# A convolution, gated token mixing and channel mixing kernel: full-width convolution matmuls, chunk stages placed by another slot, separate wave-sum tiles, fixed sum tiles

## The chip, the cores and the metric

One NeuronCore of a Trainium2 chip. The metric is the device time of the kernel in microseconds (us), the median of several executions. Instruction times come from one profiled execution of each kernel.

In the profile lines PE is TensorE, DVE VectorE, ACT ScalarE, POOL GpSimd and SP (SPq) the queue of SyncE; L424 is a line of the kernel.

## The reference

```python
# x: [8, 4224, 192]; weight: [8 heads, 7 taps]
w   = softmax(weight, over taps)
x   = causal depthwise convolution of x with w (24 channels per head)
theta = x @ w_theta                           # [192, 192]
zr, zi = x * cos(theta), x * sin(theta)
y   = w_tok_r @ zr + w_tok_i @ zi             # over tokens, [4224, 4224] each
u   = x + y
out = u + max(u @ w_ch, 0)                    # w_ch: [192, 192]
```

Nearly all the work is the two token products. The kernel does them in bf16, seven block products in place of eight per pair of row blocks (a scheme with sums of operands).

## The kernel before

A *chunk* is 128 tokens: it is convolved, transposed, multiplied with `w_theta` (the stage "theta"), turned into `zr` and `zi` ("wave"), and three sums of these are made for the seven products. Eleven chunks are resident in SBUF; 33 pass through. A *visit* is one pair of 128-row blocks of the output against the resident chunks: 14 series of 11 matmuls of 384 columns (8 series in an unpaired visit, of which there is one in every 17). Partial results go to DRAM in f32 quarters and come back in *sum tiles* `d`. Everything is issued in an order that the program works out beforehand from a model of time; the unit `n` in it is the time of one fourteenth (in an unpaired visit one eighth) of a visit, 1.79 us.

The convolution of a chunk, two 64-column halves side by side in one bank:

```python
for hh in range(2):
    h = 2 * hp + hh
    for half in range(2):
        pe(nc.tensor.matmul(
            pc[half * 2 * Q : (half + 1) * 2 * Q, hh * B * G : (hh + 1) * B * G],   # Q = 32
            lhsT=bands[:, h, :, :].rearrange("p a m -> p (a m)"),                   # 96 x 64
            rhs=self.xw[:, half, :, h * G : (h + 1) * G],                           # 96 x 192
            start=True, stop=True,
        ), B * G / 2)
```

The order of a late chunk's stages (cut), as offsets from the visit before its first:

```python
zr, zi = (10.05, 12.05) if pair(visits[v][0]) else (4.05, 8.05)
for at, fn in (
    (-4.0, lambda: chunks[c].conv(0)),
    ...                                         # conv(1), conv(2), conv(3) to -2.5
    (-2.4, lambda: c + 2 < NCH and load_chunk(c + 2)),
    (-2.0, lambda: chunks[c].transpose(0)),     # DMA transposes on the SP queue
    (-1.9, lambda: chunks[c].transpose(1)),
    (-1.8, lambda: chunks[c].keep()),
    (zr - 5.0, lambda: chunks[c].theta(0)),
    ...
    (zi + 2.0, lambda: (chunks[c].sum(2), chunks[c].sum(3))),
):
    events.append((t0 + at * n, fn))
```

The sums of weights S1 to S4 are made on VectorE out of transposed weights A11 to A22, at these slots of a visit (over 14: in the visit that uses them):

```python
SLOT = {"A11": 2.4, "A21": 4.4, "A22": 6.5, "A12": 8.5,
        "S3": 14.1, "S1": 14.6, "S2": 15.3, "S4": 17.1}
```

Sum tiles come from a rotating pool of seven; `tags` counts the free ones, and two more are added late:

```python
def load(self, q, tag):
    d = dpool.tile([P, HN], F32, name="d", tag="d") if tag is None else tag
    self.d[q], self.tag[q] = d, tag
    if self.first: return
    nc.sync.dma_start(out=d, in_=part[self.u][q][:, :])
    if self.v == residual_at[self.u]:
        ...            # some us later: GpSimd adds the residual, d = d + xr (128 x 768, f32)
tags = [None] * 7
def free_sums(tag): tags.append(tag); load_sums()
```

The finished rows are transposed by DMA (ACT queue) and multiplied with `w_ch` 11 us of model time later; only the last four visits transpose them on TensorE:

```python
outputs.append((pos[0] + 11.0, self, q, transposed(ub, False, uT)))
```

Of the kernel before, what the change touches and what calls it, by code (L numbers as in the profile page):

```python
# [11 lines left out]
BF16 = mybir.dt.bfloat16  # L12
# [4 lines left out]
def kernel(  # L17
# [22 lines left out]
    nc = tc.nc  # L40
# [36 lines left out]
    def pe(ins, cols=0):  # L77
        clock[0] += cols / 2400 + 0.0025
        return in_order("pe", ins)
# [10 lines left out]
    zpool = ctx.enter_context(tc.tile_pool(name="zpool", bufs=SLOTS))  # L90
    wpool = ctx.enter_context(tc.tile_pool(name="wpool", bufs=6))
    spool = ctx.enter_context(tc.tile_pool(name="spool", bufs=4))
    dpool = ctx.enter_context(tc.tile_pool(name="dpool", bufs=7))
    BANKS = {"y": 6, "mm": 2}
    psum = {
        k: ctx.enter_context(
# [61 lines left out]
        return (a * NCH + c) * Q  # L158


    wsb = constp.tile([P, H, KS], F32, name="wsb")
    nc.sync.dma_start(out=wsb, in_=weight.partition_broadcast(P))
    half_pi = constp.tile([P, 1], F32, name="half_pi")
    nc.gpsimd.memset(half_pi, math.pi / 2)
    bands = constp.tile([2 * WR, H, 2, Q], BF16, name="bands")

    def channel_weights(w, name):
        R = D - P
# [10 lines left out]
    class Chunk:  # L179
# [23 lines left out]
        def conv(self, hp):  # L203
            if hp == 0:
                self.xz = wk.tile([P, B, D], BF16, name="xz", tag="xz")
            pc = bank("mm", "pc")
            for hh in range(2):
                h = 2 * hp + hh
                for half in range(2):
                    pe(nc.tensor.matmul(  # L210
                        pc[half * 2 * Q : (half + 1) * 2 * Q,
                           hh * B * G : (hh + 1) * B * G],
                        lhsT=bands[:, h, :, :].rearrange("p a m -> p (a m)"),
                        rhs=self.xw[:, half, :, h * G : (h + 1) * G],
                        start=True, stop=True,
                    ), B * G / 2)
            act(nc.scalar.activation(  # L217
                out=self.xz[:, :, hp * 2 * G : (hp + 1) * 2 * G].rearrange(
                    "p b (h g) -> p h b g", h=2
                ),  # L220
                in_=pc[:, 0 : 2 * B * G].rearrange("p (h b g) -> p h b g", h=2, b=B),
                func=AT.Copy,
            ))
            if hp == H // 2 - 1:
                self.xf = self.xz[:, :, :].rearrange("p b d -> p (b d)")
                self.xT, self.ang = [], []

        def keep(self):
            for a in range(NQ):
# [33 lines left out]
            ))  # L263

        def sum(self, i):
            if i == 0:
                self.zt = zpool.tile(
                    [P, 3, HN], BF16, name="zt", tag="zt", bufs=SLOTS + 1
                )
                zs[self.c] = self  # L270
            near, far = slice(0, HN), slice(HN, N)
            t = [self.zt[:, k, :] for k in range(3)]
            o, p, q = (
                lambda: (t[0], self.zr[:, far], self.zr[:, near]),
                lambda: (t[1], self.zi[:, far], t[0]),
                lambda: (self.zr[:, far], self.zi[:, far], self.zr[:, far]),
                lambda: (t[2], self.zi[:, near], t[1]),
            )[i]()
            dve(nc.vector.tensor_tensor(out=o, in0=p, in1=q, op=ALU.subtract))

        def operand(self, i, g):
            near = slice(g * PC, (g + 1) * PC)
            far = slice(HN + g * PC, HN + (g + 1) * PC)
            return {
                "B11": lambda: self.zr[:, near], "T3": lambda: self.zr[:, far],
                "B21": lambda: self.zi[:, near], "B22": lambda: self.zi[:, far],
                "T1": lambda: self.zt[:, 0, near], "T2": lambda: self.zt[:, 1, near],
                "T4": lambda: self.zt[:, 2, near],
            }[i]()

    def transposed(u, by_pe, uT=None):
# [91 lines left out]
    class Visit:  # L383
        def __init__(self, v):
            self.v = v
            self.u, self.lo, self.hi = visits[v]
            self.first, self.final = firsts[v], finals[v]
            self.pair = pair(self.u)
            self.quarters = [3, 1, 0, 2] if self.pair else [1, 0]
            self.d, self.tag, self.missing = {}, {}, set()  # L390

        def load(self, q, tag):
            d = dpool.tile([P, HN], F32, name="d", tag="d") if tag is None else tag
            self.d[q], self.tag[q] = d, tag
            if self.first:
                return
            nc.sync.dma_start(out=d, in_=part[self.u][q][:, :])
            if self.v == residual_at[self.u]:
                self.missing.add(q)
                later(4.0, lambda: self.residual(q))  # L400
# [31 lines left out]
        def add(self, q, y, g, begins=False, ends=False):  # L432
            while q not in self.d or q in self.missing:
                if delayed:
                    delayed.pop(0)[2]()
                else:
                    output_step()
            o = self.d[q][:, g * PC : (g + 1) * PC]
            if self.first and begins:
                act(nc.scalar.activation(out=o, in_=y[:, 0:PC], func=AT.Copy))  # L440
            else:
                dve(nc.vector.tensor_tensor(out=o, in0=y[:, 0:PC], in1=o, op=ALU.add))  # L442
            if not (ends and g == NG - 1):
                return
            if self.final:
                self.output(q)
                return

            def store():
                nc.sync.dma_start(out=part[self.u][q][:, :], in_=self.d[q])  # L450
                stored.add((self.u, q, self.hi))
                later(8.0, lambda: free_sums(self.tag[q]))

            later(3.0, store)

# [70 lines left out]
        def output_end(self, q, uT):  # L526
            d = self.d[q]
            for k in range(2):
                dk = d[:, k * PC : (k + 1) * PC]
                dve(nc.vector.scalar_tensor_tensor(  # L530
                    out=dk, in0=channel_mix(uT, k, wch_[0]), scalar=0.0, in1=dk,
                    op0=ALU.max, op1=ALU.add,
                ))
            bs = slice(q % 2 * B // 2, (q % 2 + 1) * B // 2)

            def store():
                nc.sync.dma_start(
                    out=out[bs, self.rows(q), :].rearrange("b s d -> s b d"),
                    in_=d[:, :].rearrange("p (b d) -> p b d", d=D),
                )  # L540
                later(8.0, lambda: free_sums(self.tag[q]))

            later(2.0, store)

# [6 lines left out]
    def later(us, fn):  # L551
        delayed.append((pos[0] + us, len(made), fn))
        made.append(None)
        delayed.sort(key=lambda x: x[:2])

    made = []
    turn = [0]
    tags = [None] * 7
    order = [Visit(v) for v in sequence]
    waiting = [(vi, q) for vi in order for q in vi.quarters]  # L560

    def free_sums(tag):
        tags.append(tag)
        load_sums()
# [36 lines left out]
    for a, lo in ((0, True), (1, False)):  # L601
# [2 lines left out]
            channel_multiplier=-1 if lo else 1, base=WR - 1 if lo else -WR,  # L604
            compare_op=ALU.is_ge, fill=0.0,
        )
    wmax = constp.tile([P, H], F32, name="wmax")
    nc.vector.tensor_reduce(out=wmax, in_=wsb, axis=mybir.AxisListType.X, op=ALU.max)
    nc.vector.tensor_tensor(
        out=wsb, in0=wsb, in1=wmax[:, :].unsqueeze(2).to_broadcast([P, H, KS]),  # L610
# [1 line left out]
    )  # L612
    nc.scalar.activation(out=wsb, in_=wsb, func=AT.Exp)
    nc.scalar.activation(out=wmax[:, 0:1], in_=wsb[:, 0, 0:1], func=AT.Sin)
    wsum = constp.tile([P, H], F32, name="wsum")
    nc.vector.tensor_reduce(out=wsum, in_=wsb, axis=mybir.AxisListType.X, op=ALU.add)
    nc.vector.tensor_scalar_add(out=wsum, in0=wsum, scalar1=1e-9)
    wrcp = constp.tile([P, H], F32, name="wrcp")
    nc.vector.reciprocal(out=wrcp, in_=wsum)
    wbf = constp.tile([P, H, KS], BF16, name="wbf")  # L620
    nc.vector.tensor_tensor(
        out=wbf, in0=wsb, in1=wrcp[:, :].unsqueeze(2).to_broadcast([P, H, KS]),
        op=ALU.mult,
# [16 lines left out]
            )  # L640
    for a in range(2):
        nc.vector.tensor_scalar_mul(
            out=bands[:, :, a, :], in0=btmp[:, 0], scalar1=block[:, a : a + 1]
        )
    ident = constp.tile([P, P], BF16, name="ident")
    make_identity(nc, ident)
# [30 lines left out]
    def chunk_events(c, v):  # L677
        t0, n = starts[v], length(v) / parts(visits[v][0])
        zr, zi = (10.05, 12.05) if pair(visits[v][0]) else (4.05, 8.05)
        for at, fn in (  # L680
            (-4.0, lambda: chunks[c].conv(0)),
            (-3.5, lambda: chunks[c].conv(1)),
            (-3.0, lambda: chunks[c].conv(2)),
            (-2.5, lambda: (chunks[c].conv(3), c == NCH - 1 and last_conv())),
            (-2.4, lambda: c + 2 < NCH and load_chunk(c + 2)),
            (-2.0, lambda: chunks[c].transpose(0)),
            (-1.9, lambda: chunks[c].transpose(1)),
            (-1.8, lambda: chunks[c].keep()),
            (zr - 5.0, lambda: chunks[c].theta(0)),
            (zr - 2.7, lambda: chunks[c].theta(1)),  # L690
            (zr, lambda: chunks[c].wave(0, 0)),
# [4 lines left out]
            (zi + 0.05, lambda: chunks[c].wave(1, 1)),  # L696
            (zi + 0.7, lambda: chunks[c].times_x(1, 0)),
            (zi + 1.2, lambda: (chunks[c].times_x(1, 1), chunks[c].sum(1))),
            (zi + 2.0, lambda: (chunks[c].sum(2), chunks[c].sum(3))),
        ):  # L700
            events.append((t0 + at * n, fn))

# [24 lines left out]
    for c in range(NCH):  # L727
# [6 lines left out]


    SLOT = {
        "A11": 2.4, "A21": 4.4, "A22": 6.5, "A12": 8.5,
        "S3": 14.1, "S1": 14.6, "S2": 15.3, "S4": 17.1,
    }
    due = []  # L740
    for v in range(len(visits)):
# [90 lines left out]
```

## Time and profile before

| | before |
|---|---|
| median of 3 runs | 1500.6 us (1495.73 to 1501.69) |
| span of the profiled run | 1498.3 us, mean granted TensorE clock 0.982 |
| TensorE busy | 1433.8 us (96%) |
| one large matmul (128x384), from the start of one to the next | 162.5 ns |

From the page of before: the busy time of each engine (us, share of the span, instructions), and the chain of work that ended last, by engine.

```profile
PE 1433.8 (96%) x9486; PEld 869.3 (58%) x9486; DVE 1101.9 (74%) x1834; ACT 336.0 (22%) x582; POOL 744.9 (50%) x1242
...
PE 78%; DMA 8%; DVE 5%; issue 2%; POOL 1%; ACT 0%; ACTq 0%; SPq 0%; DVEq 0%; POOLq 0%
```

TensorE (PE) is the bound; the other engines matter only where PE waits for them. So the next question is what PE waits for. The waits of PE in before: line, what it waited for, us in total, times, the longest.

```profile
PE v L312 <- DMA ubT<-ubT: 13.6, 5, 4.4
PE v L312 <- DMA uT<-xz: 8.7, 2, 4.4
...
PE s L424 <- DVE w L373: 4.7, 7, 1.2
...
PE y L424 <- DVE w L373: 0.5, 1, 0.5
```

The timeline of PE in before around the second wait for `uT` (start, length, instructions; in brackets the idle time before and its releaser), and the same place in windows of 1 us: window, length, PE busy (instructions), granted clock, DMA share, GB/s.

```profile
804.03 2.11 PE L424 MATMUL y<-zt,w 128*128 128x384 bf16 x12
810.39 1.46 PE L312 MATMUL v<-wth,uT 128*128 128x192 bf16 x8 [4.25 <-DMA uT<-xz]
811.64 3.41 PE L424 MATMUL y<-zt,w 128*128 128x384 bf16 x10
```

```profile
808.00:809.00 1.00, 0.00 (x0) 1.00 1.44 186
809.00:810.00 1.00, 0.00 (x0) 0.53 1.18 224
810.00:811.00 1.00, 0.61 (x4) 0.50 1.17 260
...
815.00:816.00 1.00, 1.00 (x5) 0.56 0.00 0
816.00:817.00 1.00, 1.00 (x9) 1.00 0.49 190
```

The wait costs twice: 4.25 us of idle time, and then half the clock. Ten large matmuls take 3.41 us behind it. A busy share would not show the second part: PE is "busy" at half speed.

The timeline of PE in before at a convolution:

```profile
798.98 0.36 PE L210 MATMUL pc<-xw,bands 96*64 96x192 bf16 x4
799.27 1.15 PE L424 MATMUL s<-zi,w 128*128 128x384 bf16 x6
800.35 0.36 PE L210 MATMUL pc<-xw,bands 96*64 96x192 bf16 x4
800.63 0.99 PE L424 MATMUL s<-zi,w 128*128 128x384 bf16 x5
```

Read it from start to start: from 799.27 to 800.35 are 1.08 us, but six large matmuls are 0.975; so about 0.1 us pass before a group of four. From the group's start to the next matmul it is another 0.28 to 0.29. A group costs 0.39 us.

### The profile page before, as it was taken

What the parts mean: (1) busy time and instruction counts of PE and PEld (TensorE: products, weight loads), DVE (VectorE), ACT (ScalarE), POOL (GpSimd) and SP (SyncE); (2) the same over time, 40 slices, a digit from 0 to 9 for tenths busy, and PEclk for the clock granted to TensorE, in tenths of its full rate; (3) what the DMA queues carried; (4) which work ended last, traced back from release to release, by engine and by line L of the source; (5) the groups of instructions that cost most, each with busy time, mean ns of one, the idle gap of its engine ahead of it and who ended that gap; (6) DMA issues with size and microseconds to landing.
All of it is one profiled execution on the core that took longest, in us unless ns stands there. A gap on an engine that the chain in (4) does not pass through costs nothing.

```text
span 1498.3 us, 25757 instructions
## 1 busy us (share of the span) xinstructions
PE 1433.8 (96%) x9486; PEld 869.3 (58%) x9486; DVE 1101.9 (74%) x1834; ACT 336.0 (22%) x582; POOL 744.9 (50%) x1242
## 2 busy tenths in 40 slices
PE   5899999998999999999998999999999998998988
PEld 3456666664565565566665556556556555565655
DVE  6998755443887887886764888788797867676798
ACT  4654322122212212110000211211211211111222
POOL 9885343333444553542742654454366563653560
PEclk8999999999999999999999999999999998999999
DMA  8999875757999999998897999999898999999995
GB/s 107 236 237 195 173 145 110 132 122 164 213 227 215 200 254 209 215 218 176 208 205 171 197 246 224 213 241 217 200 228 151 256 200 211 210 243 196 232 211 160
DMA packets 348782, 298.53 MB, mean 199 GB/s; under 512 B 168208, under 2 KB 295184, under 8 KB 348656
## 3 DMA queue, kind: packets, MB, share of 16 engines
q0 software_dynamic: 178496, 97.84, 50.9%
q1 hardware_dynamic: 130160, 189.21, 41.1%
q10 hardware_dynamic: 40000, 9.84, 5.0%
q8 instruction: 74, 1.21, 0.3%
q14 instruction: 52, 0.43, 0.1%
HBM read 250.21 MB, written 106.56 MB: 238 GB/s over the span
## 4 chain that ended last, share of the span: by engine, by line
PE 78%; DMA 8%; DVE 5%; issue 2%; POOL 1%; ACT 0%; ACTq 0%; SPq 0%; DVEq 0%; POOLq 0%
PE y L424 30%; PE x L424 20%; PE s L424 20%; PE v L312 4%; DMA ubT<-ubT 3%; PE pc L210 2%; DMA out_dram<-d 2%; DVE w L373 1%; DVE w L358 1%; DVE d L442 1%; DMA uT<-xz 1%; DMA xr<-xs 1%; DMA d<-part 1%; DMA st<-in_moe_w_tok_i_dram 1%; PE tp L300 1%
## 5 line engine op out<-in xcount | busy, mean ns | idle before, releaser
L424 PEld LDWEIGHTS <-w 128*128 128x128 bf16 x7572 | 731.1, 98 | 489.5 <-issue 12.8
L336 POOL DMA_DIRECT2D st<-in_moe_w_tok_r_dram x476 | 258.6, 560 | 368.3 <-DVE w L358 342.2
L358 DVE STREAM_TRANSPOSE w<-st 128x640 bf16<-128x640 bf16 (+5 forms) x416 | 336.0, 844 | 83.7 <-PE x L424 63.6
L424 PE MATMUL y<-zt,w 128*128 128x384 bf16 x2154 | 381.9, 328 | 1.9 <-ACT y L466 1.4
L336 POOL DMA_DIRECT2D st<-in_moe_w_tok_i_dram x476 | 257.5, 555 | 147.1 <-DVE w L358 111.0
L442 DVE TENSOR_TENSOR d<-y,d 128x384 f32<-128x384 f32 x266 | 143.8, 545 | 118.7 <-PE y L424 106.9
L424 PE MATMUL x<-zr,w 128*128 128x384 bf16 x1110 | 199.9, 333 | 0.0
L424 PE MATMUL x<-zi,w 128*128 128x384 bf16 x1110 | 199.3, 327 | 0.0
L424 PE MATMUL s<-zi,w 128*128 128x384 bf16 x1044 | 191.8, 327 | 0.0
L373 DVE TENSOR_TENSOR w<-w 128x1408 bf16<-128x1408 bf16 (+10 forms) x220 | 185.7, 844 | 3.2
L424 PE MATMUL s<-zt,w 128*128 128x384 bf16 x1044 | 182.4, 327 | 4.9 <-DVE w L373 4.7
L424 PE MATMUL y<-zr,w 128*128 128x384 bf16 x1044 | 180.9, 326 | 0.1
L408 POOL TENSOR_TENSOR d<-d,xr 128x768 f32<-128x768 f32 x61 | 101.9, 1673 | 127.6 <-DMA d<-part 53.1
L442 DVE TENSOR_TENSOR d<-s,d 128x384 f32<-128x384 f32 x186 | 101.6, 548 | 67.4 <-PE s L424 66.2
L217 ACT ACTIVATE xz<-pc 128x384 bf16<-128x384 f32 x132 | 64.6, 492 | 357.1 <-PE pc L210 276.6
L466 ACT ACTIVATE y<-x 128x384 f32<-128x384 f32 x116 | 54.9, 475 | 319.0 <-PE x L424 306.1
L198 POOL DMA_DIRECT2D xw<-in_x_dram x132 | 76.9, 601 | 53.6 <-PE pc L210 37.0
L241 DVE TENSOR_SCALAR ang<-v 128x384 f32<-128x384 f32 x132 | 67.3, 547 | 27.3 <-PE v L312 26.9
L312 PEld LDWEIGHTS <-uT 128*128 128x128 bf16 x632 | 56.4, 101 | 28.0 <-DMA uT<-xz 9.5
L312 PE MATMUL v<-wth,uT 128*128 128x192 bf16 x528 | 58.5, 255 | 11.8 <-DMA uT<-xz 8.7
L514 ACT ACTIVATE ubT<-d 128x768 bf16<-128x768 f32 x41 | 34.6, 843 | 155.8 <-DVE d L442 131.5
L253 ACT ACTIVATE zr<-ang,half_pi 128x768 bf16<-128x768 f32 x66 | 59.0, 927 | 31.3 <-PE y L424 27.4
(82 smaller groups left out, 778.3 us busy)
## 6 DMA issues: line engine op xcount, KB each, us to landing
part<-d SPq DMA_DIRECT2D x171, 384.0 KB, 4.2
d<-part SPq DMA_DIRECT2D x156, 384.0 KB, 4.6
st<-in_moe_w_tok_r_dram POOLq DMA_DIRECT2D x316, 88.0 KB, 4.3
st<-in_moe_w_tok_i_dram POOLq DMA_DIRECT2D x316, 88.0 KB, 3.9
out_dram<-d SPq DMA_DIRECT2D x51, 384.0 KB, 4.9
xs<-xz SPq DMA_DIRECT2D x132, 96.0 KB, 3.0
xr<-xs POOLq DMA_DIRECT2D x66, 192.0 KB, 4.6
xw<-in_x_dram POOLq DMA_DIRECT2D x129, 96.0 KB, 4.8
```

The costliest lines, as they stand in the source:

```text
L198: nc.gpsimd.dma_start(out=self.xw[lo : lo + n, h, :, :], in_=x[:, t0 : t0 + n, :].rearrange("b s d -> s b d"),)
L217: act(nc.scalar.activation(out=self.xz[:, :, hp * 2 * G : (hp + 1) * 2 * G].rearrange("p b (h g) -> p h b g", h=2), in_=pc[:, 0 : 2 * B * ...
L241: dve(nc.vector.tensor_scalar(out=af[:, k * 2 * D : (k + 1) * 2 * D], in0=channel_mix(self.xT[g], k, wth), scalar1=-CLAMP, scalar2=CLAMP, ...
L253: act(nc.scalar.activation(out=z[:, g * HN : (g + 1) * HN], in_=self.ang[g], func=AT.Sin, **({"bias": half_pi[:], "scale": 1.0} if i == 0 ...
L312: pe(nc.tensor.matmul(v[:, b * D : (b + 1) * D], lhsT=tT[:, 3 * k + b + i, :], rhs=w[:, 2 * b + i, :], start=(i == 0), stop=(i == 1),), D)
L336: nc.gpsimd.dma_start(out=st[a * Q : (a + 1) * Q, :, 0 : self.n * Q], in_=w[t * P : (t + 1) * P, t0 : t0 + self.n * Q].rearrange("(bt i) s ...
L358: dve(nc.vector.transpose(w[:, c:ce, :, :], st[:, :, c * Q : ce * Q].rearrange("p bt (c j) -> p c bt j", j=Q),))
L373: dve(nc.vector.tensor_tensor(out=flat(o), in0=flat(self.w[p]), in1=flat(self.w[q]), op=op))
L408: nc.gpsimd.tensor_tensor(out=d, in0=d, in1=xr, op=ALU.add)
L424: pe(nc.tensor.matmul(y[:, 0:PC], lhsT=self.w.block(a, c), rhs=zs[c].operand(b, g), start=(start and c == self.lo), stop=(c == self.hi - 1 ...
L442: dve(nc.vector.tensor_tensor(out=o, in0=y[:, 0:PC], in1=o, op=ALU.add))
L466: act(nc.scalar.activation(out=y[g][:, 0:PC], in_=x[g][:, 0:PC], func=AT.Copy))
```

## The change

Its intent: place the chunk's early stages at a fixed distance ahead of its wave stage, also in an unpaired visit; replace the two half-width convolutions by full-width ones that accumulate, with zeros beside the bands; put the three wave sums into separate tiles, with one buffer less; use the SBUF that this frees for an eighth sum tile, and hand on exactly the tile that was freed; shift the slots of the weights. The core of it (setup tiles that only moved are cut):

```diff
-    dpool = ctx.enter_context(tc.tile_pool(name="dpool", bufs=7))
+    dpool = ctx.enter_context(tc.tile_pool(name="dpool", bufs=8))
...
-    bands = constp.tile([2 * WR, H, 2, Q], BF16, name="bands")
+    bands = constp.tile([2 * WR, 2 * H + 1, 2, Q], BF16, name="bands")
+    nc.vector.memset(bands, 0.0)
...
                 for half in range(2):
+                    at = 2 * h + 1 - half
                     pe(nc.tensor.matmul(
-                        pc[half * 2 * Q : (half + 1) * 2 * Q,
-                           hh * B * G : (hh + 1) * B * G],
-                        lhsT=bands[:, h, :, :].rearrange("p a m -> p (a m)"),
+                        pc[:, hh * B * G : (hh + 1) * B * G],
+                        lhsT=bands[:, at : at + 2, :, :].rearrange("p z a m -> p (z a m)"),
                         rhs=self.xw[:, half, :, h * G : (h + 1) * G],
-                        start=True, stop=True,
+                        start=(half == 0), stop=(half == 1),
                     ), B * G / 2)
...
-            if i == 0:
-                self.zt = zpool.tile([P, 3, HN], BF16, name="zt", tag="zt", bufs=SLOTS + 1)
+            if i != 2:
+                k = (0, 1, None, 2)[i]
+                self.zt[k] = zpool.tile([P, HN], BF16, name=f"zt{k}", tag=f"zt{k}")
...
-            d = dpool.tile([P, HN], F32, name="d", tag="d") if tag is None else tag
-            self.d[q], self.tag[q] = d, tag
+            self.d[q] = d = tag
...
-    tags = [None] * 7
+    tags = [dpool.tile([P, HN], F32, name="d", tag="d") for _ in range(8)]
...
-            (-4.0, lambda: chunks[c].conv(0)),          # ... conv(3) at -2.5
-            (-2.4, lambda: c + 2 < NCH and load_chunk(c + 2)),
-            (-2.0, lambda: chunks[c].transpose(0)),     # ... transpose(1), keep() to -1.8
+            (zr - 14.0, lambda: chunks[c].conv(0)),     # ... conv(3) at zr - 12.5
+            (zr - 6.0, lambda: c + 2 < NCH and load_chunk(c + 2)),
+            (zr - 12.0, lambda: chunks[c].transpose(0)),  # ... to zr - 11.8
...
-            (zi + 2.0, lambda: (chunks[c].sum(2), chunks[c].sum(3))),
+            (zi + 2.0, lambda: chunks[c].sum(2)),
+            (zi + 2.4, lambda: chunks[c].sum(3)),
...
-        "A11": 2.4, "A21": 4.4, "A22": 6.5, "A12": 8.5,
-        "S3": 14.1, "S1": 14.6, "S2": 15.3, "S4": 17.1,
+        "A11": 8.6, "A21": 4.4, "A22": 6.5, "A12": 16.0,
+        "S3": 13.6, "S1": 14.3, "S2": 15.0, "S4": 17.6,
```

In a paired visit `zr - 14.0` is -3.95, so there nearly nothing moves but the load of a later chunk; in an unpaired visit it is -9.95.

More of the change, by code (lines that the diff above doesn't have):

```diff
@@ L158, in tokens @@
         return (a * NCH + c) * Q
-    wsb = constp.tile([P, H, KS], F32, name="wsb")
+    taps_f = wk.tile([P, 4, H * KS], F32, name="taps_f", tag="xr")
+    wsb = taps_f[:, 0, :].rearrange("p (h k) -> p h k", h=H)
     nc.sync.dma_start(out=wsb, in_=weight.partition_broadcast(P))
@@ L225, in conv @@
                 self.xf = self.xz[:, :, :].rearrange("p b d -> p (b d)")
-                self.xT, self.ang = [], []
+                self.xT, self.ang, self.zt = [], [], {}
+                zs[self.c] = self
         def keep(self):
@@ L265, in sum @@
         def sum(self, i):
-            if i == 0:
-                self.zt = zpool.tile(
-                    [P, 3, HN], BF16, name="zt", tag="zt", bufs=SLOTS + 1
-                )
-                zs[self.c] = self
+            if i != 2:
+                k = (0, 1, None, 2)[i]
+                self.zt[k] = zpool.tile([P, HN], BF16, name=f"zt{k}", tag=f"zt{k}")
             near, far = slice(0, HN), slice(HN, N)
-            t = [self.zt[:, k, :] for k in range(3)]
+            t = self.zt
             o, p, q = (
@@ L286, in operand @@
                 "B21": lambda: self.zi[:, near], "B22": lambda: self.zi[:, far],
-                "T1": lambda: self.zt[:, 0, near], "T2": lambda: self.zt[:, 1, near],
-                "T4": lambda: self.zt[:, 2, near],
+                "T1": lambda: self.zt[0][:, near], "T2": lambda: self.zt[1][:, near],
+                "T4": lambda: self.zt[2][:, near],
             }[i]()
@@ L389, in __init__ @@
             self.quarters = [3, 1, 0, 2] if self.pair else [1, 0]
-            self.d, self.tag, self.missing = {}, {}, set()
+            self.d, self.missing = {}, set()
         def load(self, q, tag):
-            d = dpool.tile([P, HN], F32, name="d", tag="d") if tag is None else tag
-            self.d[q], self.tag[q] = d, tag
+            self.d[q] = d = tag
             if self.first:
@@ L451, in store @@
                 stored.add((self.u, q, self.hi))
-                later(8.0, lambda: free_sums(self.tag[q]))
+                later(8.0, lambda: free_sums(self.d[q]))
             later(3.0, store)
@@ L540, in store @@
                 )
-                later(8.0, lambda: free_sums(self.tag[q]))
+                later(8.0, lambda: free_sums(self.d[q]))
             later(2.0, store)
@@ L606 @@
         )
-    wmax = constp.tile([P, H], F32, name="wmax")
+    wmax, wsum, wrcp = (taps_f[:, 1, k * H : (k + 1) * H] for k in range(3))
     nc.vector.tensor_reduce(out=wmax, in_=wsb, axis=mybir.AxisListType.X, op=ALU.max)
@@ L614 @@
     nc.scalar.activation(out=wmax[:, 0:1], in_=wsb[:, 0, 0:1], func=AT.Sin)
-    wsum = constp.tile([P, H], F32, name="wsum")
     nc.vector.tensor_reduce(out=wsum, in_=wsb, axis=mybir.AxisListType.X, op=ALU.add)
     nc.vector.tensor_scalar_add(out=wsum, in0=wsum, scalar1=1e-9)
-    wrcp = constp.tile([P, H], F32, name="wrcp")
     nc.vector.reciprocal(out=wrcp, in_=wsum)
-    wbf = constp.tile([P, H, KS], BF16, name="wbf")
+    wbf = wk.tile([P, H, KS], BF16, name="wbf", tag="xr")
     nc.vector.tensor_tensor(
@@ L642 @@
         nc.vector.tensor_scalar_mul(
-            out=bands[:, :, a, :], in0=btmp[:, 0], scalar1=block[:, a : a + 1]
+            out=bands[:, 1 : 2 * H : 2, a, :], in0=btmp[:, 0], scalar1=block[:, a : a + 1]
         )
@@ L680, in chunk_events @@
         for at, fn in (
-            (-4.0, lambda: chunks[c].conv(0)),
-            (-3.5, lambda: chunks[c].conv(1)),
-            (-3.0, lambda: chunks[c].conv(2)),
-            (-2.5, lambda: (chunks[c].conv(3), c == NCH - 1 and last_conv())),
-            (-2.4, lambda: c + 2 < NCH and load_chunk(c + 2)),
-            (-2.0, lambda: chunks[c].transpose(0)),
-            (-1.9, lambda: chunks[c].transpose(1)),
-            (-1.8, lambda: chunks[c].keep()),
+            (zr - 14.0, lambda: chunks[c].conv(0)),
+            (zr - 13.5, lambda: chunks[c].conv(1)),
+            (zr - 13.0, lambda: chunks[c].conv(2)),
+            (zr - 12.5, lambda: (chunks[c].conv(3), c == NCH - 1 and last_conv())),
+            (zr - 6.0, lambda: c + 2 < NCH and load_chunk(c + 2)),
+            (zr - 12.0, lambda: chunks[c].transpose(0)),
+            (zr - 11.9, lambda: chunks[c].transpose(1)),
+            (zr - 11.8, lambda: chunks[c].keep()),
             (zr - 5.0, lambda: chunks[c].theta(0)),
```

## The prediction

> **What bounds it now.** TensorE: the busy table gives PE 1433.8 of 1498.3 us (96%), the chain of waits is 78% PE. In the timeline 22 large matmuls (128x384) take 3.575 us, 162.5 ns each; nothing to gain there. Time can only come from (a) 64.5 us of PE idle, (b) time at half clock (mean granted clock 0.982, about 27 us-equivalents), (c) the small matmuls. By windows of 100 us the idle time is 22 us in the start, 4.8 in 300-400, 6.1 in 800-900, about 21 in 1100-1400, 12 after 1400.
>
> **What the change does.**
>
> 1. *Chunk stages relative to the zr slot.* In an unpaired visit (half as long) convolution, DMA transposes and theta come close together: the timeline shows PE idle 4.45 us at 352 and 4.25 us at 806 for "DMA uT<-xz", the two chunks prepared in unpaired visits. The granted clock then falls to 0.50 for 6.2 us (809.4-815.6), about 5.2 of them work at half rate: 2.6 us more. The Trainium skill, "TensorE: Matmul & The Clock Gate", Part 1, says that an idle window of about 3.4 us halves the clock until the array has been busy as long; the trace agrees. The change puts transposes 7 units of 1.79 us ahead of theta instead of 1: both waits go. Gain 2 x 6.95 = 14 us, all on PE.
>
> 2. *Full-width convolution.* Now 96x64 matmuls in two column halves. The stretch 798.9-804.0, 5.15 us, minus 22 large matmuls (3.58) leaves 1.57 us for 16 convolution matmuls, 98 ns each. Full-width 192-column matmuls (v) take 82.5 ns (8 in 0.66 us). The count stays 16 per chunk. The Trainium skill, "TensorEngine Tiling (Array Packing)", Key Properties, says that switching the tiling mode drains the array; the trace shows about 0.1 us before each group of four, and hardly an overlap of the halves. Estimate 1.57 -> 1.32 us, x33 chunks, less in the start where PE isn't bound: 7 us.
>
> 3. *Order on VectorE.* PE waits for S1/S2 weight sums 5.2 us in 8 places (waits view). S1 moves ahead of the chunk's last wave sum. Gain 3 us. Rotating A11/A12 keeps the cadence of loads: 0.
>
> 4. *Eight fixed sum tiles instead of seven in rotation.* In 1150-1400 PE waits 15.6 us for the output transposes' DMA, and the clock falls (0.80 in 1237-1262, 0.83 in 1205-1215): some 20 us. The chain there runs out_dram<-d, d<-part, POOL add, ACT, DMA ubT, PE: loads wait for a tile whose store hasn't landed (SP queue: 124 us on out_dram<-d). One tile more, always the one just freed, loosens this; but the DMA engines are saturated here (share 1.0-1.18), transposes take up to 14 us, and that stays. Gain 3.5 us, the most uncertain term.
>
> 5. *Added:* a memset of the bands (about 0.6 us in VectorE's idle time), wave-sum tiles with one buffer less (slack about 1.5 slots): 0. PE waits on no wave sum today, so splitting that tile gains nothing itself. Later chunk loads free the POOL queue (37 us waiting for pc), off the path.
>
> **Predicted:** 1500.6 - 14 - 7 - 3 - 3.5 = 1473 us, range 1458 to 1487; faster by over 2% (below 1470.6) 0.42, within 2% 0.56, slower 0.02.
>
> **Right or wrong in the profile:** no PE wait "DMA uT<-xz", clock 1.00 in 300-400 and 800-900; pc matmuls 96x128, 0.33 us per group without the drain; PE wait for DVE w under 2 us; output-transpose waits after 1150 somewhat smaller; startup (0-100) within 2 us.
>
> **What would make it wrong:** the late stage (1150-1400) is a race of DMA, VectorE and PE; shifted phases can move it by 10 us either way, since a wait beyond about 3.4 us also halves the clock. The later A11/A12 slots could make early, short visits wait for weights.

## The result, and the profile after

| | before | after |
|---|---|---|
| median | 1499.63 us (4 runs) | 1476.76 us (1475.71 to 1478.46, 4 runs) |
| ratio | 1 | 0.9852 (95%: 0.9828 to 0.9875) |
| profiled span, mean clock | 1498.3 us, 0.982 | 1474.0 us, 0.990 |

A ratio here is the mean time of one kernel's fast runs over that of the other's of the same rounds, so it is not quite the ratio of the medians. Later the unchanged kernel after gave 0.9894 (0.985 to 0.9938) in another session, so the change makes the kernel 1.1 to 1.5% faster, which a threshold of 2% calls the same.

The page, and the waits of PE, of after:

```profile
PE 1418.4 (96%) x9486; PEld 898.6 (61%) x9486; DVE 1099.7 (75%) x1835; ACT 336.9 (23%) x582; POOL 745.1 (51%) x1242
...
PE 81%; DMA 10%; DVE 3%; POOL 3%; issue 2%; ACT 1%; SPq 0%; ACTq 0%; DVEq 0%; POOLq 0%
```

```profile
PE v L314 <- DMA ubT<-ubT: 11.3, 6, 3.4
...
PE s L425 <- DVE w L375: 5.5, 4, 2.2
```

The wait for `uT<-xz` is gone from the list, the wait for `ubT` is little smaller, and the wait for the sums of weights has not shrunk. The same place in the kernel as shown of before (the second unpaired visit), and a convolution, in the timeline of after:

```profile
795.60 2.11 PE L425 MATMUL y<-zt,w 128*128 128x384 bf16 x12
797.55 0.82 PE L314 MATMUL v<-wth,uT 128*128 128x192 bf16 x8
798.21 1.79 PE L425 MATMUL y<-zt,w 128*128 128x384 bf16 x10
```

```profile
333.04 0.49 PE L214 MATMUL pc<-xw,bands 96*128 96x192 bf16 x4
333.37 0.98 PE L425 MATMUL y<-zt,w 128*128 128x384 bf16 x5
334.18 0.49 PE L214 MATMUL pc<-xw,bands 96*128 96x192 bf16 x4
334.51 1.14 PE L425 MATMUL y<-zt,w 128*128 128x384 bf16 x6
```

Theta follows without a wait and the matmuls behind it run at full speed. A group of four convolution matmuls takes 0.33 us, and nothing passes before it (333.37 to 334.18 is 0.81 us, and five large matmuls are 0.8125).

**Where the time came from.** The large matmuls come in the same order in every kernel, so one can compare when the same matmul starts. I cut the kernel at the 1,601st and the 6,001st of the 7,656 recorded ones: the *start* (chunk pipeline filling up), the *steady stage* (in before 336 to 1134 us) and the *late stage* (results leave). In each I add up the idle times of PE; "work" is the rest, which includes the loss at half clock.

| us | before | after | after, again |
|---|---|---|---|
| to the 1,601st | 336.3 | 335.2 | 334.5 |
| steady stage | 798.0 | 778.3 | 777.2 |
| - its work | 785.7 | 772.9 | 773.5 |
| - idle for `uT<-xz` | 8.7 | 0 | 0 |
| - idle for the weights' sums (w) | 3.7 | 5.3 | 3.8 |
| - time at half clock | 13.7 | 0 | 0 |
| late stage (to the last large matmul) | 352.8 | 349.3 | 352.5 |

So 20 of the 24 us of the profiles are from the steady stage (about 1 us of that is an artifact: with the moved stages twelve convolution matmuls, 82.5 ns each in after, fall before the first cut). This is the measure that I use below, since the times of whole runs are too coarse for 3 to 5 us: in the last session eleven runs of before went from 1490.7 to 1508.1 us. It has one flaw: each figure is of one profile. The run "after, again" shows what repeats. A third profile is a_delay15 below, which differs from after only in the late stage: its steady stage took 780.0 us with 6.5 us of waits for w. So three profiles of one steady stage give 777.2 to 780.0 us and 3.8 to 6.5 us of waits, and smaller differences are not shown by one profile.

### The profile page after: what moved, and what is told of

Its sections match the earlier page's. It is cut to its first block, busy times and chain, and to the rows that moved or that the text cites. A ratio compares the mean times of both kernels' runs of the same rounds, so it can differ in the third digit from the quotient of the medians.

```text
span 1474.0 us, 25705 instructions
## 1 busy us (share of the span) xinstructions
PE 1418.4 (96%) x9486; PEld 898.6 (61%) x9486; DVE 1099.7 (75%) x1835; ACT 336.9 (23%) x582; POOL 745.1 (51%) x1242
## 4 chain that ended last, share of the span: by engine, by line
PE 81%; DMA 10%; DVE 3%; POOL 3%; issue 2%; ACT 1%; SPq 0%; ACTq 0%; DVEq 0%; POOLq 0%
PE y L425 31%; PE x L425 21%; PE s L425 21%; PE v L314 4%; PE pc L214 2%; DMA out_dram<-d 2%; DMA ubT<-ubT 2%; POOL st L338 2%; DMA st<-in_moe_w_tok_r_dram 2%; DVE w L375 1%; DMA st<-in_moe_w_tok_i_dram 1%; DMA out_dram<-late 1%; DMA uT<-ub 1%; DVE d L443 1%; PE tp L302 1%
## 5 line engine op out<-in xcount | busy, mean ns | idle before, releaser
L360 DVE STREAM_TRANSPOSE w<-st 128x640 bf16<-128x640 bf16 (+5 forms) x416 | 334.5, 841 | 38.1 <-PE s L425 24.2
L375 DVE TENSOR_TENSOR w<-w 128x1408 bf16<-128x1408 bf16 (+10 forms) x220 | 189.8, 863 | 1.4
L409 POOL TENSOR_TENSOR d<-d,xr 128x768 f32<-128x768 f32 x57 | 96.5, 1696 | 120.5 <-DMA d<-part 84.5
L214 PE MATMUL pc<-xw,bands 96*128 96x192 bf16 x528 | 65.4, 246 | 6.4 <-ACT xz L220 5.7
L531 DVE SCALAR_TENSOR_TENSOR d<-v,d 128x384 f32<-128x384 f32 x104 | 53.2, 548 | 21.3 <-PE v L314 20.8
```

The costliest lines, as they stand in the source:

```text
L214: pe(nc.tensor.matmul(pc[:, hh * B * G : (hh + 1) * B * G], lhsT=bands[:, at : at + 2, :, :].rearrange("p z a m -> p (z a m)"), rhs=self.x ...
L360: dve(nc.vector.transpose(w[:, c:ce, :, :], st[:, :, c * Q : ce * Q].rearrange("p bt (c j) -> p c bt j", j=Q),))
L375: dve(nc.vector.tensor_tensor(out=flat(o), in0=flat(self.w[p]), in1=flat(self.w[q]), op=op))
L409: nc.gpsimd.tensor_tensor(out=d, in0=d, in1=xr, op=ALU.add)
```

## The experiments

All outputs are right. "b_" kernels change before, "a_" kernels change after.

### One part of the change at a time

**b_stage**: only the stage lines of the diff (`zr - 14.0` to `zr - 11.8`, and the load at `zr - 6.0`).

> The kernel before with only the chunk stages placed relative to the zr slot. My theory (two transpose waits and the half clock after each are most of the gain): 14 us less than before, about 1485 us, ratio 0.9905; no PE wait for the DMA of uT in the middle of the kernel; clock 1.00 in 300-400 and 800-900. Rival (the gain is mostly in the sum tiles and the late stage, the waits would come back elsewhere): under 5 us.

Measured: 1493.47 us, ratio 0.9974 (0.9944 to 1.0003). In the profile the steady stage took 784.0 us, 14.0 less than in before: the two waits for `uT` (8.7) went, no time at half clock was left, and work fell by 6.7. (Of these 6.7, 1.2 is an artifact: twelve convolution matmuls moved ahead of the cut, at 98 ns.) The waits for w rose by 1.2. Most direct is the time between the same two large matmuls around each of the two waits (from the 1,676th to the 1,736th and from the 4,228th to the 4,288th): 18.52 and 18.17 us in before, 11.07 and 11.07 in b_stage and in after. That is 14.55 us less, where 14 were expected.

So the mechanism is right where it was expected. But the expectation for the whole run (ratio 0.9905) was missed: the interval excludes it, and the gain of about 4 us is the size that the rival named. In this profile the late stage took 357.6 us, 4.8 more; whether the gain is regularly lost there was not tested.

**b_conv**: only the convolution, with the split wave-sum tiles for room in SBUF.

```diff
-  start=True, stop=True        # two 96x64 matmuls side by side
+  start=(half == 0), stop=(half == 1)   # 96x128 with zeros, accumulating; bands and zt as in the diff
```

> The kernel before with only the full-width convolution (and the split wave-sum tiles, which it needs for room in SBUF). My theory: 0.24 us for each of 33 chunks where TensorE is the bound, 7 us less, about 1492 us, ratio 0.995; each group of four convolution matmuls costs 0.33 us in the PE timeline instead of 0.39. Rival (the groups hide behind something else, or the two column halves lose nothing): within 2 us of before.

Measured: 1500.59 us, ratio 1.0027 (1.0002 to 1.0053). No gain in time; if anything it is slower. In the steady stage work fell by 4.8 us (785.7 to 780.9) over 22 chunks, 0.22 us each, as expected; but the waits for `uT` rose from 8.7 to 11.0 and those for w from 3.7 to 7.1. What PE saved, it waited. The error was to expect the saving of one engine's work in the total, although other engines set the ends of those waits. That the waits grew because PE came earlier is my reading; no run shows it by itself.

**b_sums8**: only the eight fixed sum tiles, with the split wave-sum tiles.

```diff
-    tags = [None] * 7
+    tags = [dpool.tile([P, HN], F32, name="d", tag="d") for _ in range(8)]
```

> The kernel before with eight fixed sum tiles instead of seven in rotation (and the split wave-sum tiles, for room). My theory as on record: 3.5 us less. What I think after reading the trace of after: the late stage only trades one wait for another, so 0 to 5 us less, all of it after 1150 us, and nothing before that.

Measured: 1499.68 us, ratio 1.0011 (0.9984 to 1.0039). Late stage 352.4 us against 352.8: nothing, within what the second guess had (0 to 5 us).

**b_slot**: only the weight slots and the fourth wave sum at `zi + 2.4`.

> The kernel before with only the moved weight slots and the fourth wave sum issued later than the third. As on record: 3 us less, because PE's waits for S1 and S2 vanish. Rival, from the trace of after, where those waits are 5.5 us as before: they come from VectorE instructions that share their time with a GpSimd addition of the residual, so moving S1 by 0.3 slots only moves which visits are hit: 0, between 2 us less and 3 us more.

Measured: 1497.16 us, ratio 0.9975 (0.9941 to 1.0009). In the steady stage the waits for w fell from 3.7 to 0.7 us: alone, the slots do what the prediction said, and the rival was wrong for this surrounding. The stage as a whole was 5.4 us shorter, which is more than the waits for w: about 1.2 us come from a first spell at half clock of 3.4 us where before had 6.8, which the slots do not explain.

### Why the waits for w came back in after

In after three waits make up 5.3 us in the steady stage. VectorE and GpSimd (POOL) in after just ahead of the one at 484.15, from their timelines:

```profile
479.31 0.88 DVE L375 TENSOR_TENSOR w<-w 128x1408 bf16<-128x1408 bf16 x1
...
481.04 3.05 DVE L375 TENSOR_TENSOR w<-w 128x1408 bf16<-128x1408 bf16 x1
```

```profile
478.68 0.59 POOL L406 DMA_DIRECT2D xr<-xs  x1 [0.30 <-POOL d L409]
479.37 2.30 POOL L201 DMA_DIRECT2D xw<-in_x_dram  x4
481.68 1.65 POOL L409 TENSOR_TENSOR d<-d,xr 128x768 f32<-128x768 f32 x1
```

The same sum (S1, the second `w<-w`) takes 3.05 us where the one before it took 0.88, and it ends 0.76 us after GpSimd's addition of the residual has ended. The Trainium skill, "SBUF — State Buffer", section "SBUF: two separate sides", says that VectorE and GpSimd share a pair of SBUF ports as an exclusive lock, held for a whole instruction, and counts VectorE instructions with two SBUF inputs among those that need it. The trace agrees: of the 152 sums of this size in after, the 134 that overlap no GpSimd addition take 882 ns on average and none over 893; the 18 that do take 1679 on average, up to 3050. (In before: 139 of 883, and 13 of 1576.) The 18 fall into two kinds: ten sums ended 0.75 to 0.76 us after the addition, as if they had been held up until it was over; eight kept their 0.88 us, and the addition ended 1.5 us or more after them. So what matters for PE is also when GpSimd adds the residual, not only the slot of S1. No run moved the additions by themselves; this is read from the traces.

**a_noslot**: after with the old slots and the old place of the fourth sum.

> The kernel after with the old weight slots and the old place of the fourth wave sum. If the slots are worth the same in this surrounding as alone (6.9 us by 1134 us in the profile of the slots alone), 6 us more than after. If the waits for S1 in after undo the slots' gain, 0 to 2 us more.

Measured: 1489.07 us, ratio to before 0.991 (0.9856 to 0.9965). Steady stage 784.2 us against 777.2 to 780.0, so 4.2 to 7.0 longer; 6 was the first guess. Waits for w 8.4 against 3.8 to 6.5 in the three profiles of after, and behind one of them (2.02 us) 3.4 us at half clock. So the slots are worth something there too, but the other parts of the change had raised these waits from 3.7 to 8.4 first. Against before, nothing of these waits is saved.

**a_sums7**: after with seven fixed tiles (`bufs=7`, `range(7)`).

> The kernel after with seven fixed sum tiles instead of eight. If the eighth tile is worth the 3.5 us on record, this takes 1480 us against 1477, all of the difference after 1150 us. Rival, from the run with eight tiles alone (nothing gained): the same as after within 3 us up to 1130 us, and a late stage that differs by some us in either direction.

Measured: 1480.89 us, ratio to before 0.9849 (0.9784 to 0.9914), not to be told from after. The profile holds a surprise: waits for w in the steady stage 0.2 us, and the steady stage 772.8 us, the shortest of all. The waits for w between 335 and 1135 us in before, b_slot, after and a_sums7 (a further wait of 0.5 us in before is shown above):

```profile
PE s L424 <- DVE w L373: 3.2, 5, 1.2
PE s L424 <- DVE w L373: 0.7, 1, 0.7
PE s L425 <- DVE w L375: 5.3, 3, 2.2
PE s L425 <- DVE w L375: 0.2, 1, 0.2
```

So with the eighth tile gone these waits go. But the long sums do not: after and a_sums7 each have seven over 1 us in the steady stage. With seven tiles they fall where PE does not need the sum at once. The eighth tile is not the only part that moves them: the waits also fell to 1.6 us in a_noconv and 1.8 in a_load, and with eight tiles alone (b_sums8) they were 4.9 against 3.7. That a shifted order in time decides which sum is hit is what these profiles fit; no run shows it by itself.

In the late stage this profile took 366.7 us, 14 to 17 more than after. It is of the slowest of four runs that spread from 1470.37 to 1488.95, so whether seven tiles are really worse late is open; at their best they gave the fastest run.

**a_load**: after with the loads of the chunk after next right behind the convolution again.

```diff
-            (zr - 6.0, lambda: c + 2 < NCH and load_chunk(c + 2)),
+            (zr - 12.4, lambda: c + 2 < NCH and load_chunk(c + 2)),
```

> The kernel after, with one change more: the loads of the chunk after next are issued right behind the convolution again (before: 0.1 slots after its last group; after: 6 slots later). My theory of the S1 waits in after: the four loads (2.3 us on the GpSimd queue) stand between two additions of the residual there and push the second one into the time of the S1 sum on VectorE, which then takes 3.0 us instead of 0.9. With the loads earlier the S1 waits at about 484, 597 and 1070 us go: PE wait for DVE w 5.5 to under 2 us, 4 us less than after, about 1473. Rival (the collision doesn't depend on these loads): the waits stay, same as after.

Measured: 1486.31 us, ratio to before 0.9879 (0.982 to 0.9939). The theory of the collision held in the main (waits for w in the steady stage 5.3 to 1.8, those at 484 and 597 us gone; one of 1.5 us at 1073 stayed), the expected gain did not come: waits for `uT<-xz` came back, 6.0 us in three places, one of them with the half clock after it. In a_load, the DMA queue of SP and the timeline of PE at the longest:

```profile
870.71 0.32 SPq L398 DMA_DIRECT2D d<-part  x1
871.12 2.44 SPq L192 DMA_DIRECT2D xw<-xw  x4
873.61 2.75 SPq L298 DMA_TRANSPOSE uT<-xz  x2
```

```profile
879.66 1.36 PE L314 MATMUL v<-wth,uT 128*128 128x192 bf16 x8 [4.02 <-DMA uT<-xz]
```

The convolution's last group began at 861.79, but the transposes were issued at 873.61, behind a load of a sum tile and the copies that belong to `load_chunk`, in the same queue. The copies took 2.44 us of the queue, and the load before them had waited for a store to land. So there is a reason to put the load six slots later, as the change does: it keeps those copies out of the way of the transposes. One wait was traded for another; the steady stage took 782.9 us.

### What the convolution is worth, and by which mechanism

**a_noconv**: after with the old convolution.

> The kernel after with the old convolution in two column halves. As on record, 7 us more than after: 1484. Rival, from the run of the convolution alone, which gained nothing: within 2 us of after. In the PE timeline the chunk stretches should show 0.39 us for each group of four, so that the start of the same matmul before the late stage (about 1113 us in after) comes 5 to 8 us later.

Measured: 1481.91 us, ratio to before 0.9858 (0.9804 to 0.9913). Work in the steady stage 777.8 us against 772.9 and 773.5: 4.3 to 4.9 us for 22 chunks. Its waits for w are 1.6 us against 3.8 to 6.5, so the stage as a whole (779.4 us) is not to be told from the 777.2 to 780.0 of after. In the start, where PE waits for the chunk pipeline, the old convolution costs nothing: the cut is reached at 335.2 us, as in after.

**b_convdbl**: before with every half computed twice (`for half in (0, 1, 0, 1)`), with the same result.

> The kernel before with each half of each convolution computed twice, eight 64-column matmuls in a group instead of four (the result is the same). It separates a cost for each matmul from one for each change of the tiling. On record I took 98 ns for each matmul, with hardly any overlap of the halves: then a group costs 0.78 us. What the trace of before shows when read matmul by matmul: the two halves start 4 ns apart, the next pair 107 ns later, and some 0.09 us go before and 0.10 after each group: then a group costs 0.19 + 4 x 0.107 = 0.6 us, and full-width matmuls win only because the groups are short.

Measured, in the timeline of PE:

```profile
813.57 1.15 PE L424 MATMUL s<-zi,w 128*128 128x384 bf16 x6
814.65 0.52 PE L210 MATMUL pc<-xw,bands 96*64 96x192 bf16 x8
815.10 0.99 PE L424 MATMUL s<-zi,w 128*128 128x384 bf16 x5
...
818.83 0.49 PE L424 MATMUL y<-zt,w 128*128 128x384 bf16 x2
```

A group of eight takes 0.45 us to the next matmul and about 0.1 us before it. Over the four groups of the chunk (818.83 less 813.025, where the series before them ends, less 3.575 for the 22 large matmuls between) it is 2.23 us, 0.56 a group. Four matmuls more cost 0.165 us, 41 ns each: half of the 82.5 ns of a full-width one. So the two halves do run side by side, at full efficiency, and a group of four is 4 x 41 = 0.16 us of matmuls and a fixed 0.23 us. Full-width groups do not have the fixed part, so I put it down to changing the tiling and back; no run separates this from, say, the loading of the weights. The trace of before shows it too, matmul by matmul: the halves start 4 ns apart. My reading ("hardly an overlap of the halves", 98 ns each) had the right sum and the wrong parts. The whole run took 1519.83 us (one run, state unknown) for 528 matmuls more, 21 us over the median of before in that session; 528 x 41 ns are 21.6.

### What the half clock is worth

**b_fill**: before with 18 idle matmuls ahead of theta in the two unpaired visits.

```diff
+    def fill(c):
+        f = bank("mm", "fill")
+        for _ in range(18):
+            pe(nc.tensor.matmul(f, lhsT=ident, rhs=zs[c - 1].zr[:, 0:512], start=True, stop=True), 512)
-            (zr - 5.0, lambda: chunks[c].theta(0)),
+            (zr - 5.0, lambda: (not pair(visits[v][0]) and fill(c), chunks[c].theta(0))),
```

> The kernel before with 18 idle matmuls of 512 columns (3.9 us) just ahead of the first theta of the two chunks that are prepared in unpaired visits; they write a bank that nobody reads. They fill most of the wait for the transposes and shorten nothing. If half of my 7 us each is right (2.6 us of half clock after the wait), the clock stays 1.00 in 350-365 and 805-820, the wait left is under 0.7 us, and the matmuls behind it start 2.6 us earlier than in before, each time, in the profile (5 us in all). Rival (the clock costs nothing, only the wait does): no gain.

Measured, in the timeline of PE at the first of the two:

```profile
352.15 4.05 PE L680 MATMUL fill<-zr,ident 128*128 128x512 bf16 x18
356.87 0.83 PE L312 MATMUL v<-wth,uT 128*128 128x192 bf16 x8 [0.67 <-DMA uT<-xz]
357.54 1.79 PE L424 MATMUL y<-zt,w 128*128 128x384 bf16 x10
```

The windows of 100 us of before and of b_fill (window, length; then busy us and instructions of PE, PEld, DVE, ACT and POOL; granted clock, DMA share, GB/s):

```profile
300.00:400.00 100.00, 95.16 (x600) 55.73 (x597) 49.80 (x74) 22.38 (x43) 42.22 (x70) 0.97 0.77 156
800.00:900.00 100.00, 93.87 (x608) 54.40 (x607) 74.66 (x113) 19.32 (x33) 52.20 (x82) 0.97 1.05 214
```

```profile
300.00:400.00 100.00, 98.81 (x634) 57.32 (x633) 52.99 (x78) 23.45 (x45) 42.37 (x70) 1.00 0.78 158
800.00:900.00 100.00, 97.56 (x640) 56.67 (x639) 75.89 (x118) 18.82 (x32) 55.95 (x86) 1.00 1.08 221
```

Matmuls of no use, and nothing else, keep the clock at 1.00 and make the ten large matmuls behind the wait take 1.79 us again. Between the same two large matmuls as above it takes 15.79 and 15.93 us where before takes 18.52 and 18.17: 5.0 us less in all, as expected. (The steady stage took 793.8 us against 798.0.) (The run of 1498.78 us is a single one of state unknown and decides nothing at this size.)

### The late stage

**a_delay15**: after with the product of the output 15 us behind its transpose instead of 11.

```diff
-  outputs.append((pos[0] + 11.0, self, q, transposed(ub, False, uT)))
+  outputs.append((pos[0] + 15.0, self, q, transposed(ub, False, uT)))
```

> The kernel after with the products of the output scheduled 15 us behind their DMA transpose instead of 11. My theory of the late stage: the transposes take up to 13 us from issue to landing there, so 11 us are too few, and each miss costs the wait and some half clock; with 15 the PE waits for ubT and uT, 13.8 us in after, fall under 5, and 8 us go: about 1469, better than both. Rival: the chain through the stores of the output, the sum tiles and their loads sets the pace, and tiles held 4 us longer make it worse: same or up to 8 us more than after.

Measured: 1479.71 us, ratio to before 0.9892 (0.985 to 0.9934); after in the same session 1477.78 and 0.9894. PE's waits after 1135 us in after, and in a_delay15:

```profile
PE v L314 <- DMA ubT<-ubT: 11.3, 6, 3.4
PE y L425 <- ACT y L467: 6.4, 4, 2.4
PE v L314 <- DMA uT<-ub: 2.5, 1, 2.5
```

```profile
PE y L425 <- DVE d L443: 9.3, 1, 9.3
PE v L314 <- DVE d L531: 6.7, 4, 5.5
PE y L425 <- ACT y L467: 4.4, 5, 1.3
```

The waits for the transposes vanish altogether, and waits for VectorE's additions into `d` take their place; the late stage took 350.2 us against 349.3 and 352.5. So the length of the transposes is not what limits this stage. What does was not settled: that tiles held longer delay the loads behind them is the likely link, but no run shows it by itself.

**after_again**: the kernel after, unchanged, once more.

> The kernel after once more, unchanged, to see what of a profile repeats and how far the times of one kernel spread beside those of the others. Theory: up to 1113 us the same within 2 us, with S1 waits again at about 484, 597 and 1070 us, because engines and queues in order bring the same collisions; after that the late stage differs by up to 5 us or more, because it depends on when DMAs land. Ratio to before 0.985 within 0.004. If the S1 waits sit elsewhere, the earlier comparisons by single profiles are worth less than I take them for.

Measured: 1477.78 us (1476.61 to 1488.67), ratio 0.9894 (0.985 to 0.9938). Waits for w again at 483.1 and 595.4 us, and at 846 (0.33), not at 1070. At the 6,001st large matmul it was 1.7 us ahead of the first profile; in the late stage it was 3.2 us longer. So, with a_delay15, the steady stage is good to about 3 us from one profile, and differences of 3 us in the late stage mean nothing. The expected ratio, 0.985 within 0.004, was just missed.

No version clearly beat after. Seven fixed tiles had the shortest steady stage, in one profile; a better late stage for them is open.

## Why the prediction was right, point by point

The total, 1473 us with a range of 1458 to 1487, holds the 1476.76 us measured. Its terms fared differently, so that the sum came out so near is in part luck: of 27.5 us in four terms, the first is shown, and the other three did not arrive as forecast.

1. *Chunk stages, 14 us.* Right in mechanism and size. Around the two waits b_stage and after are 14.55 us shorter; 8.7 are the waits, and b_fill shows the half clock by itself (5.0 us). In whole-run times this part alone brought only about 4 us. The predicted signs (no wait for `uT<-xz`, clock 1.00 in both windows) are all there. The Trainium skill, "TensorE: Matmul & The Clock Gate", Part 1, is borne out in kind: idle from 806.1 us, clock 0.50 from about 809, back at 815.9.
2. *Convolution, 7 us.* The cost on PE was right (0.33 us per group, 4.3 to 4.9 us over 22 chunks; over the first 11 no gain shows in time). What arrives in the steady stage is not clear of the spread (a_noconv: 779.4 against 777.2 to 780.0), since waits for the weights' sums take the place of the work. The mechanism was half wrong: the halves overlap fully, and the loss is a fixed 0.23 us a group (b_convdbl).
3. *Order on VectorE, 3 us.* **This step failed**: the waits for w were 3.7 us in the steady stage before, 3.8 to 6.5 after, where under 2 were forecast. Read alone it was right (b_slot: 3.7 to 0.7), but I took the waits to come from the order of VectorE's own instructions, and overlooked that a sum takes up to 3.05 us in place of 0.88 while GpSimd adds a residual. The other parts of the change move the additions and the sums against each other: with seven tiles the waits are 0.2 us (a_sums7).
4. *Eight fixed tiles, 3.5 us, "the most uncertain term".* Not shown. Alone nothing (b_sums8: late stage 352.4 against 352.8); after's late stage was 3.5 us shorter in one profile and 0.3 in the other. And after has 3.6 to 6.3 us more waiting in the steady stage than the one profile with seven tiles (point 3).
5. *Added work, 0; startup within 2 us.* Right, by the first cut: 335.2 and 334.5 us to the cut against 336.3.

So the profile's sum is: about 14 from the stages, 4 to 5 of work from the convolution, 1 to 2 from the start, waits for w even or up to 3 more, and 0 to 3.5 late. The parts alone do not add up to it in whole-run times: the sum of the four ratios' gains is about 0.1%, against 1.5% for all together. In steady-stage times they nearly do (b_stage -14.0, b_slot -5.4, b_conv +0.9, b_sums8 +1.9: -16.6 in sum, against -18.0 to -20.8 in three profiles of after). In these profiles most of the difference lies in the late stage: it took 357.6 us in b_stage and 358.4 in b_slot, against 352.8 in before and 349.3 to 352.5 in the profiles of after and a_delay15. Why the parts together do not lose time there was not found.

## What to carry to other kernels

An engine's saving reaches the total only up to the next wait that another engine sets: count the stretch between waits, not the instructions. Look at the clock where the bound engine waits for two microseconds or more; here the half clock after two waits of 4.25 and 4.45 us cost another 5.0 us, and idle matmuls or an earlier producer both cured it. When an instruction's time varies by a factor of three, look at what the engine that shares its SBUF ports does at that moment before moving it in its own queue. Measure a part of a change in the change's own surrounding too: alone the slots cut the waits to 0.7 us, with the rest they did not.

## What the Trainium skill lacked or had wrong

- "TensorEngine Tiling (Array Packing)" says that a change of the tiling mode drains the array, but not what it costs. Here a group of matmuls in two column halves has a fixed cost of 0.23 us, which I put down to going there and back, against 41 ns for each 192-column matmul in a half; with four matmuls to a group the full-width form (4 x 82.5 ns) wins, and by these numbers (an estimate) with eight or more the halves do (0.56 against 0.66 us).
- "TensorE: Matmul & The Clock Gate" puts the idle time that halves the clock at about 3.4 us. In before a wait of 2.65 us in the late stage (ending at 1239.73 us) was enough: the clock is at half from 1239.1 us for 3.4 us. In a_noslot a single wait of 2.02 us (ending at 486.07) was followed by half clock from 487.1 for 3.4 us, while in after one of 2.40 us (ending at 1334.88) was not: no length of a single wait separates the two cases here.
- "SBUF — State Buffer" says that of VectorE and GpSimd the one that starts first gets the shared ports for its whole instruction. For 14 of the 18 overlaps in after the recorded starts agree: in six the addition is first and the sum late, in eight the sum is first and the addition late. In the other four the sum is recorded as started first, by up to 0.64 us, and still ended 0.76 us after the addition. In all four GpSimd was still issuing a DMA when the sum started, but also in two of the eight. So recorded starts are not always the order in which the ports are had (or GpSimd's times, which are rough, are off). What tells the holder here is the end: the one held up ends late, the sum by 0.75 to 0.76 us or the addition by 1.5 us or more. The page gives no such sign.
